# Two attention and MLP layers on one core: the last block of rows for layer 2 is turned by VectorE in 32x32 blocks and through DRAM

## The chip, the cores and the metric

The kernel runs on one core of a Trainium2 chip. The metric is the device time of one execution in microseconds (us), given as the median of several runs. The profile comes from one further execution.

Five engines appear: PE (TensorE: matmuls; PEld is its weight load), DVE (VectorE), ACT (ScalarE), POOL (GpSimd) and SP (SyncE), whose queue issues nearly all DMAs of this kernel. Each engine takes its instructions in the order in which the program lists them, and waits at one whose input is not there.

## What is computed

Two layers are applied twice with the same weights, to x of 2048 rows by 640 columns (S by D), all in float32. There are 32 heads of 20 columns, and the MLP has 1536 hidden columns.

```python
def _A_ref(x, wqkv, wo):                    # attention
    qkv = (x @ wqkv).reshape(B, S, 3, H, Dh).transpose(2, 0, 3, 1, 4)
    q, k, v = qkv[0], qkv[1], qkv[2]
    scores = jnp.einsum("bhqd,bhkd->bhqk", q, k) * (Dh ** -0.5)
    p = _softmax(scores, axis=-1)
    o = jnp.einsum("bhqk,bhkd->bhqd", p, v)
    return o.transpose(0, 2, 1, 3).reshape(B, S, D) @ wo

def _B_ref(x, w1, b1, w2, b2):              # MLP
    r = jnp.maximum(jnp.einsum("bsd,df->bsf", x, w1) + b1, 0)
    return jnp.einsum("bsf,fd->bsd", r * r, w2) + b2

x = x + _A_ref(_layernorm(x), wqkv, wo)
x = x + _B_ref(_layernorm(x), w1, b1, w2, b2)
x = x + _A_ref(_layernorm(x), wqkv, wo)
x = x + _B_ref(_layernorm(x), w1, b1, w2, b2)
```

## The kernel before

**Stages.** `layer` (L1256) is called twice. Each call runs the projections (`qkv`, L674), the attention (L941), the output projection (`add_heads`, L1125) and the MLP (`mlp`, L1195). The 2048 rows are worked on as four blocks (`tb` 0 to 3) of 512 rows, each of them four row tiles of 128 x 640.

**Turned rows.** A projection needs the normalised rows turned, with the 640 columns on partitions: five tiles `xnT` of 128 x 2 x 512, where the middle index is the high and the low part of each number. `xt_[tb]` holds the five tiles of a block. The kernel has two ways to make them:

- `front` (L376): VectorE takes the statistics of four row tiles (`stats`, L239; the last two operations of it, an addition and a power, run on POOL) and normalises them. TensorE then turns them with 20 transposes of 128x128 (L393) into banks of PSUM. Each bank is split into high and low parts, by ACT and VectorE (`split_to`) or by ACT and POOL (`split_on_pool`).
- `turn_out` and `turn_in` (L1146, L1180): VectorE normalises each row tile and turns it in 32x32 blocks (L1172), four DMAs per row tile store the blocks to their turned places in a DRAM tensor `d_t` (`store`, L1156, pieces of 128 bytes), and five DMAs load the turned block back. ACT then copies the high part (L1188) and VectorE subtracts it for the low part (L1189).

For layer 2, the blocks 0, 1 and 2 are turned the second way during the last MLP pieces of layer 1 (L1321 to L1328). Block 3 consists of the rows that this MLP writes last, in four DMAs to `d_x[1]`. Its turning is the generator `second` (L1340), and it is the first way, `front(3, ...)`.

**Projections.** `qkv` works through `UNITS`: first 16 units of queries and keys, four of each block (tb 0, then 1, 2 and 3), then the rest. Unit 0 is the keys of the first heads for block 0, unit 1 their queries, unit 2 keys again. A unit has 30 matmuls (L322) of half the rows of the array each. The halves are issued in pairs, so 15 turns of the inner loop (L890 to L897) issue what one unit needs. The two halves lag each other: unit 0 is complete after turn 30, unit 1 after turn 45, unit 2 after 60, and so on. A complete unit is copied out of PSUM by ACT (L263) and split by POOL (L268, L271) into a tile `ev`. The store of `ev` to `d_qk` (`thrice`, two DMAs of 512 and 256 KB) is put on SP's queue one unit later: that of unit 0 at turn 45, of unit 1 at turn 60, of unit 2 at turn 75. ACT also makes a small mark (L324) after each first half of a unit, for which the second half waits.

**Maxima.** The softmax needs row maxima of the scores. A part of them is put between the projections: `by_queries` (L474) multiplies a tile `q` with a tile `k`, loaded back from `d_qk`, and VectorE reduces the result (L486). The loads of the first `k` and `q` (`tiles`, two DMAs each) go on SP's queue at turn 75, right behind the store of unit 2. The first of these matmuls comes at turn 105, ahead of unit 7's first. The `q` tile holds what unit 1 gave, so its load waits for unit 1's store.

**The order of the steps.** The generator that makes block 3 is asked for its next step (`step_rest`, L826) on every fourth turn of the inner loop. Each step yields a cost in us by which a small model of the engines' times is moved on, and a flag. With the flag set, the next step is made only when two PSUM banks are free. The model decides where the maxima go. `front` has 12 steps, and puts its last transposes on the queues some 50 turns in. If `xt_[3]` is not there when unit 12 is due, all remaining steps are made at once (L887). Unit 12 is the first to use it.

Of the kernel before, what the change touches and what calls it, by code (L numbers as in the profile page):

```python
# [39 lines left out]
def tile_layers(  # L40
# [26 lines left out]
    def slot(shape, dtype, label):  # L67
        return arena.tile(shape, dtype, tag="slot", name=name(label))

    def dma(eng, dst, src):  # L70

        if dst.dtype == F32R:
            dst = dst.bitcast(F32)
        if src.dtype == F32R:
            src = src.bitcast(F32)
        eng.dma_start(dst, src)  # L76

    def xtile(label):
        return xpool.tile([P, D], F32, tag="x", name=name(label))
# [18 lines left out]
    ps_q = Ring(0, 1, 2, 3)  # L98
# [137 lines left out]
    d_t = [dram.tile([D, QB], F32, name=f"d_t{i}") for i in range(5)]  # L236
    d_x = [dram.tile([S, D], F32, name=f"d_x{i}") for i in range(3)]

    def stats(x):  # L239

        st = small.tile([P, 2, 6], F32, tag="bst", bufs=3, name=name("bst"))
        mv = small.tile([P, 2], F32, tag="mv", bufs=6, name=name("mv"))
        for i in range(2):
            nc.vector.bn_stats(st[:, i, :], x[:, i * HALF : (i + 1) * HALF])  # L244
        nc.vector.bn_aggr(mv, st)
        var = mv[:, 1:2]
        nc.gpsimd.tensor_tensor(var, var, eps_t, op=ALU.add)
        nc.gpsimd.tensor_tensor(var, var, half_t, op=ALU.pow)
        return mv

    def normalise(eng, x, mv):
        eng.tensor_scalar(x, x, mv[:, 0:1], mv[:, 1:2], op0=ALU.subtract, op1=ALU.mult)
# [22 lines left out]
    def row_tile(src, r):  # L275
        t = xtile("x")
        dma(nc.sync, t, src[r * P : (r + 1) * P, :])
        return t
# [11 lines left out]
    xt_, keys = {}, {}  # L290
# [85 lines left out]
    def front(tb, x_src, bank, each=1, on_pool=()):  # L376

        rows = [row_tile(x_src, tb * 4 + i) for i in range(4)]
        yield 0, False
        mvs = []  # L380
        for x in rows:
            mvs.append(stats(x))
            yield 1.1, False
        for n, (x, mv) in enumerate(zip(rows, mvs)):
            normalise(nc.vector, x, mv)
            yield 0.65, n == 3
        res = []
        for k0 in range(0, KD, each):
            ks = range(k0, min(k0 + each, KD))
            dsts = [bank("xt") for _ in ks]  # L390
            for k, dst in zip(ks, dsts):
                for i in range(4):
                    nc.tensor.transpose(  # L393
                        dst[:, i * P : (i + 1) * P], rows[i][:, k * P : (k + 1) * P], ident
                    )
            for k, dst in zip(ks, dsts):
                t = slot([P, 2, QB], F32R, "xnT")
                (split_on_pool if k in on_pool else split_to)(t[:, 0, :], t[:, 1, :], dst)
                res.append(t)
            if len(res) == KD:  # L400
                xt_[tb] = res
                rows.clear()
            yield 0, len(res) < KD
# [742 lines left out]
    def turn_out(d, xs):  # L1146

        if callable(xs):
            read, xs = xs, []
            xs.extend(read(i) for i in range(2))  # L1150
        else:
            read = None
        yield
        y = None

        def store(i):  # L1156
            for a in range(4):
                t0 = i * P + 32 * a
                dma(
                    nc.sync,  # L1160
                    d[:, t0 : t0 + 32].rearrange("(b j) t -> j b t", j=32),
                    y[32 * a : 32 * a + 32].rearrange("j (b t) -> j b t", t=32),
                )

        for i in range(4):
            if y is not None:
                store(i - 1)
            mv = stats(xs[i])
            yield
            normalise(nc.vector, xs[i], mv)  # L1170
            y = xtile("y")
            nc.vector.transpose(y, xs[i])  # L1172
            if read and i < 2:
                xs.append(read(i + 2))
            yield
        store(3)
        xs.clear()
        yield

    def turn_in(d, get, sub=nc.vector.tensor_sub):  # L1180

        res = get()
        for k in range(KD):
            dma(nc.sync, res[k][:, 1, :], d[k * P : (k + 1) * P, :])
        yield
        for k in range(KD):
            raw = res[k][:, 1, :].bitcast(F32)
            nc.scalar.copy(res[k][:, 0, :], raw)  # L1188
            sub(res[k][:, 1, :], raw, res[k][:, 0, :].bitcast(F32))  # L1189
            yield  # L1190

    def new_rows():
        return [slot([P, 2, QB], F32R, "xnT") for _ in range(KD)]
# [146 lines left out]
    def second():  # L1340


        yield from front(3, d_x[1], ps_q, 2, (1, 3))

    def constants():

# [57 lines left out]
    opening = begin_first()  # L1404
    next(opening)
    ahead = second()
    layer(True, x_in, d_x[0], d_x[1], opening, ahead)
    layer(False, d_x[1], d_x[2], x_out, ahead, None)
# [28 lines left out]
```

## Time and profile before

| what | us |
|---|---|
| median of three runs | 3612.47 |
| lowest and highest of them | 3610.52, 3614.29 |
| the profiled execution's own time | 3611.78 |
| span of its trace | 3610.0 |
| of it PE busy | 3582.4 |
| of it DVE busy | 2753.2 |
| of it ACT busy | 2640.6 |
| start of layer 2's projections in the trace | 1819.4 |
| first matmul for a maximum in layer 2 (L474) | 1849.6 |

Times in the trace count from the start of the span. The execution's own time stands 1.78 us above its span, and 0.69 us below the median. A row of the timeline gives start, length, engine, line, operation, what is written and read, and the number of instructions merged into it. In brackets stands how long the engine was idle before and what ended that. Lengths of merged rows include short waits between the instructions. "SPq" rows are DMAs being issued; their data moves later.

### The profile page before, as it was taken

How to read it: one execution, taken by the hardware profiler on the slowest of the kernel's cores; microseconds unless marked ns; L12 is line 12 of the kernel's file. 1: busy time of each engine (PE TensorE's matmuls, PEld its weight loads, DVE VectorE, ACT ScalarE, POOL GpSimd, SP SyncE). 2: the span in 40 equal slices, each digit the busy share in tenths (PEclk: the TensorE clock that was granted, in tenths of full speed). 3: DMA queues.
4: the chain of work that ended last, by engine and by line, in shares of the span. 5: the costliest groups of instructions: out<-in, count | busy, mean ns of one | idle time of the engine just before them, and what ended most of it. 6: DMA issues, size and time to landing. Idle time of an engine off the chain costs nothing.

```text
span 3610.0 us, 67661 instructions
## 1 busy us (share of the span) xinstructions
PE 3582.4 (99%) x25550; PEld 2131.8 (59%) x25550; DVE 2753.2 (76%) x5083; ACT 2640.6 (73%) x5131; POOL 820.8 (23%) x904
## 2 busy tenths in 40 slices
PE   8999999999999999999999999999999999999999
PEld 6887334343344335999988964334434343368998
DVE  7877999999999993446567789999999999824443
ACT  2678999999999996122317789999999999942221
POOL 6531334212112111111154201211211211211110
PEclk9999999999999999999999999999999999999999
DMA  8865555322222125834577652222222211367221
GB/s 269 274 228 181 169 146 160 118 69 77 53 53 52 35 91 189 283 88 112 149 253 249 205 151 67 73 73 56 77 72 62 50 39 51 106 212 249 73 79 39
DMA packets 377829, 453.89 MB, mean 126 GB/s; under 512 B 176690, under 2 KB 223538, under 8 KB 377502
## 3 DMA queue, kind: packets, MB, share of 16 engines
q1 hardware_dynamic: 376686, 447.21, 41.2%
q8 instruction: 201, 3.29, 0.4%
q10 hardware_dynamic: 816, 2.36, 0.2%
q14 instruction: 126, 1.03, 0.1%
HBM read 275.14 MB, written 174.30 MB: 125 GB/s over the span
## 4 chain that ended last, share of the span: by engine, by line
PE 95%; DMA 2%; DVE 1%; ACT 1%; issue 1%; SPq 0%; POOL 0%; ACTq 0%; DVEq 0%; POOLq 0%
PE banks L568 28%; PE banks L556 19%; PE banks L474 16%; PE banks L286 12%; PE banks L322 10%; PE banks L1225 9%; PE banks L1066 1%; DMA q<-d_qk 0%; ACT e L563 0%; SPq L76 0%; DMA w<-d_w 0%; PE banks L393 0%; ACT e L1073 0%; DMA d_t<-y 0%; DVE bst L244 0%
## 5 line engine op out<-in xcount | busy, mean ns | idle before, releaser
L563 ACT ACTIVATE e<-banks 128x512 f32<-128x512 f32 x3968 | 2049.1, 603 | 66.0 <-PE banks L474 7.2
L486 DVE TENSOR_REDUCE mx<-banks 128x1 f32<-128x512 f32 x3076 | 1930.9, 684 | 213.4 <-PE banks L474 142.4
L474 PE MATMUL banks<-k,q 60*128 60x512 f32 x3587 | 1244.7, 428 | 2.7 <-DVE mx L486 1.4
L556 PE MATMUL banks<-q,k 62*128 62x512 f32 x3968 | 1117.8, 433 | 1.0 <-DVE mx L503 0.3
L568 PE MATMUL banks<-e,vg 128*32 128x512 f32 x8192 | 1091.8, 605 | 1.5 <-ACT e L1073 1.5
L556 PEld LDWEIGHTS banks<-q,k 62*128 62x128 f32 x3968 | 583.8, 185 | 657.8 <-ACT e L563 625.5
L474 PEld LDWEIGHTS banks<-k,q 60*128 60x128 f32 x3587 | 582.5, 185 | 289.5 <-DVE mx L486 216.1
L503 DVE CUSTOM_DVE_ANT_0 rl<-banks,rl 128x512 f32<-128x512 f32 x511 | 333.6, 689 | 102.1 <-PE banks L474 92.8
L322 PE MATMUL banks<-xnT,wqk 64*128 64x512 f32 x2400 | 383.4, 397 | 4.0 <-DVE xnT L257 1.8
L568 PEld LDWEIGHTS banks<-e,vg 128*32 128x32 f32 x8192 | 161.2, 108 | 357.4 <-issue 330.8
L1210 ACT ACTIVATE r<-banks,b_t 128x512 f32<-128x512 f32 x96 | 66.2, 689 | 398.0 <-PE banks L286 396.6
L495 ACT ACTIVATE rl<-banks 128x512 f32<-128x512 f32 x515 | 273.8, 597 | 102.3 <-PE banks L474 97.4
L1225 PE MATMUL banks<-w,h 128*128 128x320 f32 x2304 | 340.4, 309 | 0.0
L1225 PEld LDWEIGHTS banks<-w,h 128*128 128x128 f32 x2304 | 339.2, 188 | 1.3
L286 PE MATMUL banks<-xnT,w 128*128 128x512 f32 x1440 | 329.4, 389 | 0.0
L322 PEld LDWEIGHTS banks<-xnT,wqk 64*128 64x128 f32 x2400 | 289.7, 187 | 39.4 <-issue 2.2
L286 PEld LDWEIGHTS banks<-xnT,w 128*128 128x128 f32 x1440 | 269.6, 188 | 55.3
L268 POOL CAST mr<-nt 128x32 fp32r<-128x32 f32 x64 | 13.5, 211 | 1125.8 <-DVE nt L529 1125.7
L612 POOL TENSOR_TENSOR few<-few,minus_t 128x16 f32<-128x16 f32 x62 | 179.9, 2902 | 234.4 <-DMA few<-d_s 232.7
L322 PE MATMUL banks<-wv,xnT 64*128 64x320 f32 x1920 | 199.7, 307 | 0.9 <-ACT mark_t L324 0.9
L322 PEld LDWEIGHTS banks<-wv,xnT 64*128 64x128 f32 x1920 | 187.9, 185 | 2.7 <-ACT mark_t L324 1.6
L1211 DVE TENSOR_TENSOR r<-r 128x512 f32<-128x512 f32 x96 | 77.7, 809 | 124.7 <-ACT r L1210 124.6
(82 smaller groups left out, 2010.6 us busy)
## 6 DMA issues: line engine op xcount, KB each, us to landing
q<-d_qk SPq DMA_DIRECT2D x242, 240.0 KB
d_qk<-ev SPq DMA_DIRECT2D x80, 512.0 KB
k<-d_qk SPq DMA_DIRECT2D x152, 240.0 KB
x<-d_x SPq DMA_DIRECT2D x88, 320.0 KB
d_qk<-ev SPq DMA_DIRECT2D x80, 256.0 KB
d_o<-ot SPq DMA_DIRECT2D x248, 80.0 KB
ot<-d_o SPq DMA_DIRECT2D x38, 512.0 KB
d_v<-v SPq DMA_DIRECT2D x32, 512.0 KB
```

The source lines that it names most:

```text
L286: nc.tensor.matmul(dst, a, b, start=(n == 0), stop=(n == last))
L322: m = nc.tensor.matmul(ch["dst"][:, :width], *pair, start=first, stop=last)
L474: nc.tensor.matmul(dst, q_t[t][b : b + 60, p, sub * P : (sub + 1) * P], k_t[t // NQB, c][b : b + 60, p, :], start=True, stop=True,)
L486: nc.vector.tensor_reduce(maxima(t)[:, 2 * par + p, sub, c : c + 1], dst, axis=AX.X, op=ALU.max)
L495: nc.scalar.activation(res, dst, AF.Relu)
L503: nc.vector.tensor_tensor_reduce(out=r, in0=dst, in1=r, scale=1.0, scalar=LEAST, op0=ALU.add, op1=ALU.max, accum_out=maxima(t)[:, 2 * par ...
L556: nc.tensor.matmul(dst, k_t[t // NQB, kt // 4][b : b + 62, p, (kt % 4) * P : (kt % 4 + 1) * P], q_t[t][b : b + 62, p, :], start=True, stop ...
L563: nc.scalar.activation(es[p][:, par, :], dst, AF.Exp, scale=SCALE)
L568: nc.tensor.matmul(acc[32 * h : 32 * h + 32, :], v_t[t // NQB, kt // 8][:, kt % 8, 32 * h : 32 * h + 32], es[p][:, par, :], start=(kt == 0 ...
L612: nc.gpsimd.tensor_tensor(few, few, minus_t, op=ALU.pow)
L1211: nc.vector.tensor_mul(r, r, r)
L1225: nc.tensor.matmul(dst[:, :HALF], hs[f][:, hx, i * P : (i + 1) * P], w_2.piece(at_2(f0 + f, hw, hf)), start=(f == 0 and (hx, hw) == THREE[0]),
```

## The change

`second` no longer calls `front`. Block 3 is turned in the way of the other three blocks. The steps are spread over the same turns of the inner loop, one on every fourth turn.

```diff
     def second():
-        yield from front(3, d_x[1], ps_q, 2, (1, 3))
+        rows_out = turn_out(d_t[0], lambda i: row_tile(d_x[1], 12 + i))
+        for n, _ in enumerate(rows_out):
+            yield (0 if n in (0, 9) else 1.1 if n % 2 else 1.5), False
+        for _ in range(3):
+            yield 0, False
+        res = []
+
+        def get():
+            res.extend(new_rows())
+            return res
+
+        rows_in = turn_in(d_t[0], get)
+        next(rows_in)
+        for _ in range(6):
+            yield 0, False
+        for _ in rows_in:
+            yield 0.7, False
+        xt_[3] = res
+        yield 0, False
```

The new `second` has 25 steps, all with the flag off. With one step on every fourth turn, they fall as follows:

| turn | step |
|---|---|
| 4 | two row loads |
| 8, 16, 24, 32 | statistics of row tiles 0 to 3; those at 16, 24 and 32 are preceded by the four stores of the tile before |
| 12, 20, 28, 36 | normalise and turn row tiles 0 to 3; row loads 2 and 3 at turns 12 and 20 |
| 40 | the four stores of row tile 3 |
| 44, 48, 52 | nothing |
| 56 | the five loads of the turned block |
| 60 to 76 | nothing |
| 80, 84, 88, 92, 96 | one ACT copy and one VectorE subtraction each |
| 100 | `xt_[3]` is set |

## The prediction

> **What bounds the kernel now.** I read the page first.
>
> ```profile
> PE 3582.4 (99%) x25550; PEld 2131.8 (59%) x25550; DVE 2753.2 (76%) x5083; ACT 2640.6 (73%) x5131; POOL 820.8 (23%) x904
> PE 95%; DMA 2%; DVE 1%; ACT 1%; issue 1%; SPq 0%; POOL 0%; ACTq 0%; DVEq 0%; POOLq 0%
> ```
>
> PE is busy nearly always and holds 95% of the chain that ended last. So a stretch that PE loses or gains ends up in the total, unless something else then holds PE up. The change touches the first units of layer 2's projections. The table by windows, for the projection matmuls alone, shows PE's time there.
>
> ```profile
> 1819.30:1829.07 9.77, 9.20 (x72) 6.78 (x72) 1.00 0.47 168
> 1829.07:1836.07 7.00, 3.20 (x22) 1.72 (x20) 1.00 0.30 115
> 1836.07:1849.36 13.29, 13.29 (x118) 10.98 (x119) 1.00 0.63 204
> ```
>
> The columns are the window, its length, busy time of PE and PEld with counts, granted clock, DMA share and GB/s. The timeline of PE fills in the middle window.
>
> ```profile
> 1829.08 0.64 PE L393 MATMUL banks<-ident,x 128*128 128x128 f32 x3
> 1830.21 0.77 PE L393 MATMUL banks<-ident,x 128*128 128x128 f32 x5 [0.49 <-DVE x L252]
> 1830.90 0.50 PE L322 MATMUL banks<-xnT,wqk 64*128 64x512 f32 x2
> 1831.33 1.09 PE L393 MATMUL banks<-ident,x 128*128 128x128 f32 x8
> 1832.36 0.73 PE L322 MATMUL banks<-xnT,wqk 64*128 64x512 f32 x4
> 1833.02 0.66 PE L393 MATMUL banks<-ident,x 128*128 128x128 f32 x4
> 1833.60 1.89 PE L322 MATMUL banks<-xnT,wqk 64*128 64x512 f32 x13
> 1836.07 1.20 PE L322 MATMUL banks<-xnT,wqk 64*128 64x512 f32 x8 [0.58 <-ACT r L263]
> ```
>
> The 20 transposes, the waits between them and the late copy of a unit (0.58 us, ACT was busy with the turned banks) fill the window beside 19 projection matmuls (2+4+13).
>
> **What it removes.** A projection matmul takes 13.29/118 = 0.113 us, so 19 take 2.1 us of the 7.0. The rest, **4.9 us**, is PE time that goes with the transposes. PE would then come to the first matmul for a maximum (turn 105) at 1849.4 - 4.9 = 1844.5. This is worth something only if that matmul's data is there. In the kernel before it is just there:
>
> ```profile
> 1838.09 0.88 SPq L76 DMA_DIRECT2D d_qk<-ev  x2
> 1842.25 0.80 SPq L76 DMA_DIRECT2D d_qk<-ev  x2
> 1843.21 1.38 SPq L76 DMA_DIRECT2D k<-d_qk  x2
> 1844.71 0.85 SPq L76 DMA_DIRECT2D q<-d_qk  x2
> 1849.58 0.39 PE L474 MATMUL banks<-k,q 60*128 60x512 f32 x1
> 1850.21 0.69 PE L474 MATMUL banks<-k,q 60*128 60x512 f32 x3 [0.24 <-DMA q<-d_qk]
> ```
>
> The stores are those of units 1 and 2. The query tile's two halves are issued from 1844.71 to 1845.56, and the second ends a wait of PE at 1850.2. So **the query load is already next in line** behind PE, and the question is what the change does to it.
>
> **What it adds: the row chain.** One row tile's period on VectorE is seen where the second way runs with little else between:
>
> ```profile
> 1451.58 0.87 DVE L244 BATCH_NORM_STATS2 bst<-x 128x6 f32<-128x320 f32 x2
> 1455.42 0.86 DVE L244 BATCH_NORM_STATS2 bst<-x 128x6 f32<-128x320 f32 x2
> 1456.32 0.21 DVE L245 BATCH_NORM_AGGREGATE mv<-bst 128x2 f32<-128x12 f32 x1
> 1456.45 0.44 DVE L1140 TENSOR_TENSOR x<-banks,x 128x320 f32<-128x320 f32 x1
> 1457.46 0.61 DVE L252 TENSOR_SCALAR x<-x,mv 128x640 f32<-128x640 f32 x1 [0.57 <-POOL mv L248]
> 1458.11 0.85 DVE L1172 STREAM_TRANSPOSE y<-x 128x640 f32<-128x640 f32 x1
> 1823.55 0.89 DVE L244 BATCH_NORM_STATS2 bst<-x 128x6 f32<-128x320 f32 x2 [3.57 <-DMA x<-d_x]
> ```
>
> The period is 3.84 us. Of the two additions of L1140 in it, the one after a transpose costs 0.38 and the one after the aggregate lies under the wait for POOL, so here it is 3.46 us, and 3.54 us from statistics to the end of the transpose. The rows come as before, the first at 1823.55, because the row loads keep their place on SP. The last transpose ends at 1823.55 + 3 x 3.46 + 3.54 = 1837.5. All this lies under PE, and VectorE has no maxima yet, so it costs nothing by itself.
>
> **The stores and loads on SP.** Rows from the MLP of layer 1:
>
> ```profile
> 1773.20 1.98 SPq L76 DMA_DIRECT2D d_t<-y  x4
> 1775.29 4.76 SPq L76 DMA_DIRECT2D xnT<-d_t  x10
> 1774.00:1776.45 2.45, 2.45 (x19) 2.45 (x18) 1.24 (x3) 0.00 (x0) 0.00 (x0) 1.00 0.93 136
> 1776.45:1785.40 8.95, 8.95 (x44) 7.64 (x44) 1.88 (x3) 1.87 (x3) 0.00 (x0) 1.00 1.01 359
> ```
>
> The four stores of a row tile take 2.0 us to issue, and their data has moved 3.25 us after the first issue (1773.20 to 1776.45), 80 KB each at a mere 136 GB/s.
>
> Here the last four are issued 1837.5 to 1839.5 and have landed by about 1841.0 (3.25 and some 0.2 for the signal). Unit 0's store (turn 45) goes out between. Then come the five loads (turn 56), which need all sixteen stores. **SP waits at the first of them until 1841.0**, and issues the five by 1843.4 (4.76/10 each). Queued behind them on SP are, in this order: unit 1's store, unit 2's store, the first k and q. Before, unit 1's store went out at 1838.09. Now it goes out at 1843.4, though its tile is ready at about 1838 (POOL works on unit 0 only after the third tile's power, but that ends at 1832.5, and the units follow at 2 us each).
>
> **The query load.** It needs unit 1's store landed, and the data of all these DMAs shares the same 16 engines in order. The rate is seen where they queue:
>
> ```profile
> 1843.00:1850.10 7.10, 6.97 (x62) 5.43 (x58) 0.06 (x1) 1.69 (x6) 4.85 (x5) 1.00 0.98 309
> 1850.10:1862.00 11.90, 10.76 (x87) 9.89 (x89) 10.97 (x19) 1.98 (x5) 10.02 (x12) 1.00 0.98 334
> ```
>
> So 309 to 359 GB/s; I take 335. From 1840.75: unit 0's store (786 KB, 2.35 us), five loads (1311 KB, 3.9), unit 1's store (2.35) to 1849.3, unit 2's (2.35), k (492 KB, 1.45) to 1853.1, the first half of q (246 KB, 0.75) to 1853.9. At 359 and 309 GB/s it is 1853.0 and 1855.0. Against 1849.4 the first maximum's matmul is **3.6 to 5.6 us late; I take 4.4**, near the middle, as both rates occur within one stretch. The gain of 4.9 is eaten, since PE waits from 1844.5 to about 1853.8. ACT's five copies (turns 80 to 96) wait for the loads and hold the marks and copies of units 4 to 6 behind them, which would stop PE for some 2 us. That lies under the longer wait.
>
> **The clock.** Nine idle microseconds of PE have one more price. The table by windows shows a shorter one in layer 1:
>
> ```profile
> 83.95:87.36 3.41, 1.40 (x12) 1.36 (x14) 1.06 (x2) 1.43 (x4) 2.02 (x3) 1.00 1.04 344
> 87.36:90.77 3.41, 3.41 (x19) 3.19 (x18) 2.24 (x6) 0.44 (x1) 0.00 (x0) 0.50 1.00 381
> 90.77:94.19 3.42, 3.42 (x30) 3.24 (x30) 2.79 (x6) 1.78 (x4) 1.03 (x2) 1.00 1.06 266
> ```
>
> After a stretch of 3.41 us with PE busy for 1.40, the granted clock is 0.50 for the next one, and back at 1.00 after it; 19 matmuls ran instead of 30. The Trainium skill, "TensorE: Matmul & The Clock Gate", Part 1, halves the clock after at least one idle window of about 3.4 us; here 2.0 idle of 3.41 did it. By that page's 3.4 us to full clock, the loss would be an estimated 1.7 us.
>
> PE restarts inside a stretch at half speed, and that one or the next as well is slow: 0 to 5.4 us at half, a loss of 0 to 2.7. Behind it stands a DMA queue that is full (0.98 at 334 GB/s above) and holds PE up anyway at one place:
>
> ```profile
> 1860.16 0.47 PE L474 MATMUL banks<-k,q 60*128 60x512 f32 x1 [0.92 <-DMA q<-d_qk]
> ```
>
> That wait shrinks when PE is slow. I take 1.2 us net.
>
> **What changes nothing.** The steps after turn 105 are the same, since both generators have ended by then and the model's engines are idle again. The tb 3 tiles are ready near 1848.5 and first used by unit 12, which started at about 1874: no stall. Four transposes and three more subtractions on VectorE lie in a stretch where it is mostly idle; if maxima were there, they would cost up to 4 x 0.85 + 2 x 0.7 us.
>
> **Sum.** 3611.78 + 4.4 + 1.2 = 3617.4 for an execution like the profiled one. That one is 0.7 us under the median, so for the median I say **3618.0**. The bounds are +3.6 to +5.6, and 0 to +2.7, so 3616 to 3621.
>
> **Rivals.**
>
> 1. *The cover holds.* If the loads do not hold up the queue so, because SP gets past them early or their data moves beside unit 1's store, the query comes when unit 2's store lets it. That could be 2.2 us earlier than before (POOL done at 1840 and not 1842.2), or as early as PE wants it, 4.9. Time 3607.6 to 3610.3. For it: the DMA engines were empty for much of 1826 to 1843. The Trainium skill, "DMA: Bandwidth & Descriptors", Rules for kernel authors, says to issue a DMA early, compute, and wait late, as the fixed cost overlaps; by that rule this rival wins. Against it: the loads wait on SP, and issue is not early for what stands behind them. 15%.
> 2. *No difference.* The delay just equals what PE had lost: the query comes at 1849 to 1851, with a short cold stretch. Time 3611 to 3614. It needs the row chain to end 3 us sooner than I have it; VectorE's rows above speak against that. 12%.
> 3. *Slower still.* After the wait, the full DMA queue never makes up, and PE at half speed for two stretches loses 2.7 with no wait to absorb it. The next query tile is late too, by 1 to 3 us. Time 3611.8 + 5.6 + 2.7 + 1 to 3 + 0.7 = 3622 to 3624. It decides when the restart falls late in a stretch and the queue stays at 0.98 up to 1890. 20%.
> 4. *It does not do what it says*: block 3 is needed before it is there, and all steps are forced together ahead of unit 12. Unit 12 is due 25 us after the tiles, so under 1%.
>
> **Chances.** My forecast, 3614 to 3622 with its own slack, has 53%. From 3610 to 3623 leaves out most of the first rival and half of the third, about 2 in 10. The bound of 0.2% (7.2 us, about what a measurement of this kernel can tell from no change) lies at 3605.3 and 3619.7. Faster than that needs more than all of PE's gain: 0.04. Slower: the third rival and the upper quarter of the forecast, 0.33. The rest, 0.63, is within.
>
> **What would show it.** In the changed kernel, right would be: no L393 in layer 2; the last transpose near 1837.5; SP's loads `xnT<-d_t` near 1841, unit 1's store after them; PE idle of 8 to 10 us ahead of the first L474, ended by DMA q; a granted clock of 0.50 in the windows right after. It would be wrong if unit 1's store went out near 1838, if L474 came by 1846, or if ACT's copies, and not the query, ended PE's wait.

## The result, and the profile after

| | kernel before | changed kernel |
|---|---|---|
| median of 15 runs each, us | 3612.36 | 3619.1 |
| lowest and highest | 3607.55, 3618.24 | 3615.76, 3622.17 |
| span of the profiled execution | 3610.0 | 3617.3 |

The ratio is 1.002, with a 95% interval of 1.0012 to 1.0027: the change costs 6.7 us, between 4.3 and 9.8. The range of 3610 to 3623 holds it, and 3618.0 was forecast. A second series of the changed kernel, later and beside other kernels, gave 3619.41 against 3613.5, ratio 1.0018 (1.0009 to 1.0027).

The page of the changed kernel shows what was traded. PE lost 2.9 us of busy time, and the packets under 512 bytes grew from 176690 to 187266:

```profile
PE 3579.5 (99%) x25530; PEld 2127.8 (59%) x25530; DVE 2758.3 (76%) x5089; ACT 2639.6 (73%) x5131; POOL 815.3 (23%) x900
DMA packets 389045, 456.51 MB, mean 126 GB/s; under 512 B 187266, under 2 KB 234114, under 8 KB 388718
```

In this execution layer 2's projections start at 1816.2, against 1819.4 in the trace of before. The programs are the same up to there; the trace of before has two short stretches at half clock in layer 1 that this one lacks. So times are compared from each trace's own first projection matmul of layer 2. SP's rows in the changed kernel:

```profile
1834.86 2.14 SPq L76 DMA_DIRECT2D d_t<-y  x4
1837.11 0.95 SPq L76 DMA_DIRECT2D d_qk<-ev  x2
1839.01 2.27 SPq L76 DMA_DIRECT2D xnT<-d_t  x5
1841.33 0.94 SPq L76 DMA_DIRECT2D d_qk<-ev  x2
1842.37 2.49 SPq L76 DMA_DIRECT2D d_qk<-ev  x2
1844.95 2.21 SPq L76 DMA_DIRECT2D k<-d_qk  x2
1848.59 0.78 SPq L76 DMA_DIRECT2D q<-d_qk  x2
```

These are the last row tile's stores, unit 0's store, the five loads, the stores of units 1 and 2, the first k and the first q, in the order that the program gives. The query load goes out 32.4 us after the start (1848.59 - 1816.2); before it was 25.3 (1844.71 - 1819.4). What SP waited for between 1815 and 1849, with the total in us, the number of waits and the longest:

```profile
SPq L76 <- DVE y L1172: 8.9, 4, 5.4
SPq L76 <- DMA d_qk<-ev: 1.3, 1, 1.3
SPq L76 <- DMA d_t<-y: 0.8, 1, 0.8
```

The stores wait for VectorE's turned tiles, the loads for the stores, and the query load for unit 1's store to land. SP's queue is taken in order, so each of these waits also holds what stands behind it. PE's timeline around it, and the one further wait of note:

```profile
1828.81 13.89 PE L322 MATMUL banks<-xnT,wqk 64*128 64x512 f32 x119 [0.61 <-ACT r L263]
1853.38 1.77 PE L474 MATMUL banks<-k,q 60*128 60x512 f32 x4 [10.68 <-DMA q<-d_qk]
1885.76 0.54 PE L474 MATMUL banks<-kd,q 60*128 60x512 f32 x1 [1.88 <-DMA q<-d_qk]
```

PE is done with its seven units at about 1842.7 and waits 10.7 us for the query. The first maximum's matmul comes at 37.2 us after the start, against 30.2 before. The table by windows shows the stretch, with the granted clock before the last two columns:

```profile
1842.60:1845.06 2.46, 0.10 (x1) 0.00 (x0) 1.29 (x2) 0.62 (x1) 0.00 (x0) 1.00 0.98 287
1845.06:1853.35 8.29, 0.00 (x0) 0.00 (x0) 3.13 (x4) 2.79 (x7) 6.68 (x7) 0.50 1.03 348
1853.35:1858.71 5.36, 5.33 (x23) 4.11 (x25) 3.85 (x7) 0.00 (x0) 0.99 (x1) 0.50 1.02 402
1858.71:1883.90 25.19, 24.94 (x211) 21.27 (x207) 24.29 (x41) 4.09 (x12) 12.87 (x14) 1.00 0.94 294
1883.90:1886.00 2.10, 0.24 (x2) 0.27 (x4) 0.28 (x1) 0.00 (x0) 1.61 (x2) 1.00 1.01 380
1886.00:1889.40 3.40, 3.40 (x18) 3.08 (x18) 0.70 (x2) 1.19 (x2) 0.00 (x0) 0.50 1.02 402
```

The DMA engines are full (0.94 to 1.03) the whole time, also while PE stands still. The clock is halved from 1845.06 to 1858.71, 5.4 us of it after PE's restart, and once more after the short wait.

### The profile page after: what moved, and what is told of

It is laid out like the page before. It is cut to its first block, busy times and chain, and to the rows that moved or that the text cites. A ratio compares the mean times of both kernels' runs of the same rounds, so it can differ in the third digit from the quotient of the medians.

```text
span 3617.3 us, 67664 instructions
## 1 busy us (share of the span) xinstructions
PE 3579.5 (99%) x25530; PEld 2127.8 (59%) x25530; DVE 2758.3 (76%) x5089; ACT 2639.6 (73%) x5131; POOL 815.3 (23%) x900
## 2 busy tenths in 40 slices
DMA packets 389045, 456.51 MB, mean 126 GB/s; under 512 B 187266, under 2 KB 234114, under 8 KB 388718
## 3 DMA queue, kind: packets, MB, share of 16 engines
q14 instruction: 126, 1.03, 0.1%
## 4 chain that ended last, share of the span: by engine, by line
PE 55%; DMA 2%; issue 1%; SPq 1%; POOL 0%; DVE 0%; ACT 0%; POOLq 0%; DVEq 0%; ACTq 0%
PE banks L568 14%; PE banks L286 10%; PE banks L556 10%; PE banks L1225 9%; PE banks L474 8%; PE banks L322 5%; SPq L76 1%; DMA w<-d_w 1%; DMA d_t<-y 0%; DMA q<-d_qk 0%; DMA d_qk<-ev 0%; DMA d_x<-x 0%; DMA xnT<-d_t 0%; DMA o<-d_r 0%; DVE x L1140 0%
## 5 line engine op out<-in xcount | busy, mean ns | idle before, releaser
L474 PE MATMUL banks<-k,q 60*128 60x512 f32 x3587 | 1245.4, 429 | 12.3 <-DMA q<-d_qk 10.9
L568 PE MATMUL banks<-e,vg 128*32 128x512 f32 x8192 | 1091.0, 605 | 1.5 <-ACT e L1073 1.5
L474 PEld LDWEIGHTS banks<-k,q 60*128 60x128 f32 x3587 | 582.9, 185 | 299.9 <-DVE mx L486 217.1
L568 PEld LDWEIGHTS banks<-e,vg 128*32 128x32 f32 x8192 | 161.1, 108 | 357.5 <-issue 331.0
```

The lines of the kernel that those rows point to most:

```text
L474: nc.tensor.matmul(dst, q_t[t][b : b + 60, p, sub * P : (sub + 1) * P], k_t[t // NQB, c][b : b + 60, p, :], start=True, stop=True,)
L568: nc.tensor.matmul(acc[32 * h : 32 * h + 32, :], v_t[t // NQB, kt // 8][:, kt % 8, 32 * h : 32 * h + 32], es[p][:, par, :], start=(kt == 0 ...
```

## The experiments

The theory at this point: the stores and loads of the turned block stand in the DMA queue ahead of the first query tile, so PE waits for the query, and the transposes that it saved are worth nothing. Rivals: SP's order and not the bytes; ACT held at the copies; the halved clock.

All results in one table. "First maximum" and "attention" are the first L474 and the first L568 of layer 2, in us after its first projection matmul (from the source views of each trace, good to 0.1 us). Medians and ratios are against the kernel before in the same series.

| kernel | first maximum | attention | median, us | before, us | ratio, 95% interval |
|---|---|---|---|---|---|
| before | 30.2 | 296.9 | | | |
| changed | 37.2 | 307.8 | 3619.1 | 3612.36 | 1.002, 1.0012 to 1.0027 |
| changed, again | 37.3 | 306.0 | 3619.41 | 3613.5 | 1.0018, 1.0009 to 1.0027 |
| loads behind q | 33.2 | 305.3 | 3616.49 | 3611.56 | 1.0013, 1.0004 to 1.0021 |
| loads between | 37.2 | 306.0 | 3620.81 | 3611.56 | 1.0025, 1.0015 to 1.0036 |
| copies late | 36.7 | 307.3 | 3620.86 | 3611.56 | 1.0025, 1.0016 to 1.0034 |
| PE kept busy | 37.4 | 305.6 | 3620.14 | 3611.56 | 1.002, 1.001 to 1.003 |
| no turning | 26.2 | 294.5 | 3606.77 | 3612.52 | 0.9982, 0.9973 to 0.9991 |
| no stores | 31.0 | 299.6 | 3612.28 | 3612.52 | 1.0004, 0.9996 to 1.0013 |
| no loads | 32.5 | 301.3 | 3614.49 | 3612.52 | 1.001, 1.0001 to 1.0019 |
| PE work added | 34.5 | 300.8 | 3612.85 | 3612.52 | 1.0003, 0.9994 to 1.0012 |
| front spaced | 30.4 | 298.1 | 3612.45 | 3613.5 | 0.9995, 0.9987 to 1.0004 |
| last stores behind q | 29.5 | 303.7 | 3620.28 | 3613.5 | 1.0018, 1.0009 to 1.0027 |
| subtractions on POOL | 29.2 | 303.5 | 3614.83 | 3611.65 | 1.0012, 1.0003 to 1.0021 |

An interval is some 6 us wide, and each trace is one execution. So the places of the loss are read from the traces, and totals are compared only where intervals part.

**Loads behind the query.**

```diff
-        for _ in range(3):
+        for _ in range(8):
...
-        for _ in range(6):
+        for _ in range(10):
...
-            yield 0.7, False
+            yield 0, False
```

> The five loads of the turned block go on SP's queue at turn 76, behind the first k and q, and the copies at turns 120 to 136; the copies' cost in the model is 0, so that PE's order stays as it was. Theory (the loads stand ahead of unit 1's store and the first query load): the first maximum's matmul comes 27 to 29.5 us after layer 2's first projection matmul (30.2 before the change, 37.2 after it), no half clock; the time is 3 us under to 3 us over the kernel before, so 4 to 10 under the changed one. Rival (the loads' bytes have to pass the full DMA queue somewhere, whatever their place): the first matmul is early too, but later query loads are late by 4 us, and the time is 5 to 7 us over the kernel before.

The first maximum came at 33.2, about half way back and 3.7 us later than the latest expected. (With ten steps between, the copies fall on turns 116 to 132.) The time was 4.9 us over the kernel before, close to the rival. SP's rows and PE's waits in that kernel:

```profile
1836.12 2.14 SPq L76 DMA_DIRECT2D d_t<-y  x4
1838.36 4.66 SPq L76 DMA_DIRECT2D d_qk<-ev  x6
1843.19 1.85 SPq L76 DMA_DIRECT2D k<-d_qk  x2
1845.15 0.89 SPq L76 DMA_DIRECT2D q<-d_qk  x2
1846.08 2.37 SPq L76 DMA_DIRECT2D xnT<-d_t  x5
...
1850.53 0.76 PE L474 MATMUL banks<-k,q 60*128 60x512 f32 x1 [6.73 <-DMA q<-d_qk]
...
1884.96 0.47 PE L474 MATMUL banks<-kd,q 60*128 60x512 f32 x1 [1.33 <-DMA q<-d_qk]
```

Even with the loads out of the way, the query goes out at 27.9 (1845.15 - 1817.3) and not at 25.3. The stores, which were still ahead, keep it back, by their bytes or by SP's waits for them.

**Loads between the stores of units 1 and 2.** As above, with `range(5)` for the first number, and the second left at 6.

> The loads go on SP's queue at turn 64, behind unit 1's store but ahead of unit 2's store, k and q; the copies' cost in the model is 0. If the bytes ahead of the query in the DMA queue set its landing: q lands at most 1.5 us earlier than in the changed kernel, first maximum's matmul 35.5 to 37.5 us after the first projection matmul, time within 2 us of the changed kernel. If it is the late store of unit 1, for which the query load waits on SP: 32.5 to 35 us, and 3 to 5 us under the changed kernel.

The store of unit 1 and the query both went out earlier, and the first maximum came at 37.2 as in the changed kernel. The wait of PE and the DMA engines' load over it, with the same window of the changed kernel below:

```profile
1855.56 0.76 PE L474 MATMUL banks<-k,q 60*128 60x512 f32 x1 [10.64 <-DMA q<-d_qk]
1842.00:1855.50 13.50, 2.92 (x25) 2.06 (x22) 5.59 (x6) 4.10 (x9) 7.83 (x7) 0.71 1.02 327
```

```profile
1839.90:1853.30 13.40, 2.80 (x25) 1.99 (x21) 4.51 (x6) 4.03 (x9) 6.63 (x7) 0.69 1.01 322
```

So whether unit 1's store stands ahead of the loads or behind them on SP is not what counts. The bytes ahead of the query are the same, and they move at 322 to 327 GB/s. The stores stand in the same place in both kernels, so nothing is shown here of their order.

**Copies late.** The loads stay at turn 56; the wait of six steps becomes `range(15)`, and the copies' cost 0.

> The loads stay at turn 56, the ACT copies and VectorE subtractions go from turns 80 to 96 to turns 116 to 132, behind the first maximum; their cost in the model is 0. Theory: PE's wait is for the query load, so it stays at 10 to 11 us, and the time within 1.5 us of the changed kernel. Rival (ACT, held at the copies, holds the marks and the bank copies for which PE waits): PE's wait shrinks by 2 us or more, and so does the time.

```profile
1856.34 2.09 PE L474 MATMUL banks<-k,q 60*128 60x512 f32 x4 [10.25 <-DMA q<-d_qk]
```

The wait stays, 0.4 us shorter. In the changed kernel ACT was held for 5.28 us at the first copy, but nothing of PE's waited for it in the end. This rival falls.

**PE kept busy.**

```diff
         xt_[3] = res
+        for _ in range(72):
+            nc.tensor.transpose(banks[:, 2, :P], ident, ident)
         yield 0, False
```

> The changed kernel with 72 transposes of the identity into an unused bank at turn 100, some 9.8 us of PE work with no use, so that PE is not idle in its wait. Theory: the halved clock behind the wait costs time of its own; the granted clock stays 1.00, and the time is 2 to 3.5 us under the changed kernel. Rival (PE has nothing to do at that point but wait for the full DMA queue, so its clock costs nothing): within 1 us of the changed kernel.

The first half of the expectation missed: PE still stood idle for 2.7 us, and one stretch at half speed followed. The windows of this kernel:

```profile
1844.80:1853.40 8.60, 8.60 (x77) 7.90 (x75) 5.51 (x6) 3.67 (x7) 5.21 (x5) 1.00 0.98 340
1853.40:1856.00 2.60, 0.03 (x2) 0.00 (x0) 0.00 (x0) 0.67 (x2) 2.30 (x3) 1.00 1.03 306
1856.00:1857.60 1.60, 1.34 (x9) 0.93 (x11) 1.00 (x2) 0.00 (x0) 0.20 (x1) 1.00 1.08 425
1857.60:1861.10 3.50, 3.50 (x20) 2.87 (x18) 3.31 (x6) 0.00 (x0) 0.00 (x0) 0.52 1.01 400
```

From the first maximum to the attention it took 268.2 us, against 268.7 and 270.6 in the two traces of the changed kernel, so 0.5 to 2.4 us less. The median is no better than the changed kernel's. A price of the clock between nothing and some 2 us stays open.

**No turning.** The kernel before, with `xt_[3] = list(xt_[2])` in place of `front`.

> The kernel before, with block 3 of layer 2 not turned at all: its projections use block 2's tiles, and the row loads, statistics, transposes and splits of block 3 are left out. It bounds what any cheaper turning can give. If PE's time sets the end of this stretch: about 4.9 us under the kernel before. Theory, sharpened by the first runs (the full DMA queue sets the pace of the first 90 us, so PE's time there is worth little): first maximum's matmul 28 to 30 us after the first projection matmul, and the time 0 to 3 us under the kernel before.

PE arrives at 26.2, before the 28 to 30 that was expected, and hardly waits. The time falls by 5.8 us (3.3 to 9.8), more than the theory gave and close to the 4.9 of the rival. So PE's time there is worth something when nothing is put into the DMA queue for it. This kernel also does without the row loads and the work of VectorE and POOL, so not all of the 5.8 need be PE's.

**Stores or loads alone.** The changed kernel without the sixteen stores, and without the five loads with their copies and subtractions.

> The changed kernel without the sixteen stores of the turned blocks; the loads stay and bring what an earlier block left in the DRAM tensor. It takes 1.3 MB in pieces of 128 bytes, some 10 us of the DMA engines, out of the stretch ahead of the query load. Theory of the DMA queue: first maximum's matmul at 31 to 34 us after the first projection matmul (37.2 with the stores), time 1 to 4 us over the kernel before. If the loads alone are the cost: 36 to 37 us, and 5 to 8 us over the kernel before.

> The changed kernel without the five loads, five copies and five subtractions of the turned block; the stores stay, and block 3's projections use block 2's tiles. Theory of the DMA queue: first maximum's matmul near 33 us, as with the loads behind the query (33.2), but no later query load is held up by them, so 1 to 4 us over the kernel before. If the stores cost nothing: first maximum's matmul 28 to 30 us, and the time not over that of the kernel before.

PE's first wait for the query in either, stores left out first:

```profile
1848.62 0.76 PE L474 MATMUL banks<-k,q 60*128 60x512 f32 x1 [4.54 <-DMA q<-d_qk]
```

```profile
1848.78 2.05 PE L474 MATMUL banks<-k,q 60*128 60x512 f32 x4 [5.92 <-DMA q<-d_qk]
```

Against the changed kernel (37.2), **leaving out the stores brings the first maximum 6.2 us forward, and leaving out the loads 4.7**. With either alone it still comes later than in the kernel before (31.0 and 32.5 against 30.2). So either uses up the 4.0 us that PE gains, and neither total parts from the kernel before to the faster side.

Counted from the kernel without turning (26.2), the delays are 4.8 for the loads, 6.3 for the stores and 11.0 for both. That the first two add up to the third does not show that each is time of bytes in one queue, for two reasons. First, POOL finishes unit 1's tile at different times. Its rows for units 0 and 1 in the changed kernel, and below them for unit 1 without turning:

```profile
1829.99 1.41 POOL L271 TENSOR_TENSOR ev<-kf,ev 128x512 fp32r<-128x512 f32 x1
1833.69 1.42 POOL L271 TENSOR_TENSOR ev<-r,ev 128x512 fp32r<-128x512 f32 x1
```

```profile
1830.58 1.29 POOL L271 TENSOR_TENSOR ev<-r,ev 128x512 fp32r<-128x512 f32 x1
```

Unit 1's tile, for whose store the query waits, is ready 18.9 us after the start in the changed kernel (1835.11 - 1816.2), as it is with either part left out, but 14.6 us without turning (1831.87 - 1817.3), where POOL has no statistics to wait for. A kernel with the work on rows, but neither stores nor loads, was not run.

Second, the stores act through SP's order too. In the changed kernel unit 0's tile is ready at 1831.40, but its store goes out at 1837.11, behind the stores that SP holds for VectorE. The DMA engines are not full up to there:

```profile
1826.00:1837.10 11.10, 10.49 (x91) 8.35 (x89) 6.80 (x12) 2.13 (x6) 7.35 (x11) 1.00 0.73 123
```

So how much of the stores' 6.2 us is their bytes, and how much the pile-up behind SP's waits, these runs do not show.

**PE work added.** The kernel before, with sixteen empty steps after `front` and then 36 transposes of the identity.

> The kernel before with 36 transposes of the identity into an unused bank at turn 104, right ahead of the first maximum: 4.9 us of PE work with no use, about what the change takes away. If PE sets the pace of the stretch: 4 to 5 us over the kernel before. Theory of the DMA queue: first maximum's matmul 34 to 35.5 us after the first projection matmul, but PE then waits less for the later query loads, and the time is 0 to 2.5 us over the kernel before.

The first maximum came 4.3 us later, the time by 0.3 us (from 2.2 less to 4.3 more). The trace has the attention 3.9 us later. Together with the kernel without turning, this does not settle how much a microsecond of PE is worth here; it lies between none and all.

**Front spaced.**

```diff
-        yield from front(3, d_x[1], ps_q, 2, (1, 3))
+        for n, (cost, _) in enumerate(front(3, d_x[1], ps_q, 1)):
+            yield cost, False
+            if n == 8:
+                for _ in range(3):
+                    yield 0, False
```

> The kernel before, still with TensorE's transposes, but three empty steps ahead of them, one bank on every fourth turn, flags off, and all low parts by VectorE instead of two by POOL. PE no longer waits for VectorE's normalising nor for the late bank copy, some 1.7 of the 4.9 us; the rest is the 20 transposes and stays. Theory (each saved microsecond ahead of turn 105 counts only as far as the query load comes earlier as well, and POOL now is freer for units 0 to 2): first maximum's matmul 27.5 to 29.5 us after the first projection matmul (30.2 before), time 0.5 to 3 us under the kernel before. Rival (the query load stays where it was): 30 us, and no difference.

No difference, in place or in time (ratio 0.9995, 0.9987 to 1.0004). PE's timeline shows why:

```profile
1833.76 0.65 PE L393 MATMUL banks<-ident,x 128*128 128x128 f32 x4
1834.35 1.19 PE L322 MATMUL banks<-xnT,wqk 64*128 64x512 f32 x8
1835.47 0.66 PE L393 MATMUL banks<-ident,x 128*128 128x128 f32 x4
1836.06 1.19 PE L322 MATMUL banks<-xnT,wqk 64*128 64x512 f32 x8
1837.18 0.66 PE L393 MATMUL banks<-ident,x 128*128 128x128 f32 x4
```

There are no waits, yet the period of four transposes and eight projection matmuls is 1.71 us. Eight matmuls are 0.9 of it (8 x 0.113), so four transposes cost 0.8 us and twenty cost 4.0. The waits that I counted in the kernel before were not on top of that.

**Last stores behind the query.**

```diff
             yield (0 if n in (0, 9) else 1.1 if n % 2 else 1.5), False
-        for _ in range(3):
+            if n == 8:
+                for _ in range(9):
+                    yield 0, False
+        for _ in range(5):
...
-            yield 0.7, False
+            yield 0, False
```

> The changed kernel with the last row tile's four stores at turn 76, behind unit 2's store, k and q on SP's queue, the five loads at turn 100 and the copies from turn 124; their cost in the model is 0. The first three row tiles' stores stay ahead. If the stores cost through SP's order (the last ones wait there for VectorE's transpose, ahead of unit 0's store): first maximum's matmul 26.5 to 28.5 us after the first projection matmul. If through their bytes, some 7 of 10 us of DMA time still ahead: 30 to 32 us. In both cases the loads come later into the full queue, and the time ends 0 to 5 us over the kernel before.

The first maximum came at 29.5, a little before that of the kernel before. This is between the two cases. Against the kernel with stores and no loads (32.5), the last tile's four stores cost 3.0 us by standing ahead of the query. That does not part the two: their bytes are out of the way, but SP also has one transpose less to wait for, and unit 0's store goes out 17.2 us after the start and not 20.8. The time was 6.8 us over the kernel before. A new wait stood 12 us on, put down to VectorE, whose subtractions now stood among the maxima:

```profile
1846.89 1.89 PE L474 MATMUL banks<-k,q 60*128 60x512 f32 x4 [2.99 <-DMA q<-d_qk]
...
1863.42 0.50 PE L474 MATMUL banks<-k,q 60*128 60x512 f32 x1 [4.10 <-DVE mx L468]
```

**The same, with the subtractions on POOL.** The call becomes `turn_in(d_t[0], get, nc.gpsimd.tensor_sub)`.

> The kernel with the last stores and the loads behind the query, and the five subtractions of the turned block by POOL instead of VectorE. There, PE's second wait (4.1 us) ended with VectorE, whose subtractions stood among the maxima. If VectorE was the cost: the second wait falls under 1.5 us and the time to 1 to 4 us over the kernel before. If the loads in the full DMA queue were: a wait of 3 us or more stays, now ended by the DMA of a query or key tile, and the time stays 5 to 8 us over the kernel before.

```profile
1843.48 2.03 PE L474 MATMUL banks<-k,q 60*128 60x512 f32 x4 [2.69 <-DMA q<-d_qk]
...
1860.17 0.47 PE L474 MATMUL banks<-k,q 60*128 60x512 f32 x1 [4.04 <-DMA q<-d_qk]
```

With VectorE out of it, the second wait is as long and ends with the next query tile. So **the transfers put behind the first query are waited for at the second**: 2.7 and 4.0 us, where the changed kernel waits 10.7 us at once. The time, 3.2 us over the kernel before, lies in the range that was expected if VectorE was the cost, but its interval does not part it from the kernel ahead of it. So the wait speaks for the queue, and the total does not decide. No version that was run beats the kernel before, save the one that leaves the turning out.

## Why the prediction was right, and where it was not

- *The gain of 4.9 us on PE* was about 4.0: the kernel without turning reaches its first maximum 26.2 us after the start, not 30.2. The 4.9 counted waits that the spaced kernel shows to be no extra, and one wait for a bank copy (0.61 us) stayed.
- *The row chain* held. From the first projection matmul, the last transpose was due at 18.1 and ended at 18.7; two of the four normalisings took 0.88 us and not 0.61.
- *SP waits at the loads* held as an event (the loads went out at 22.8, due at 21.6, and unit 1's store at 25.1, due at 24.0). The loads went out 4.15 us after the first of the last four stores (1839.01 - 1834.86), where the prediction had 3.25 and some 0.2 for the signal; no run shows that 0.2 by itself. As a cause unit 1's place behind the loads counted for nothing: with its store moved ahead of them, the first maximum came no sooner. That SP waits at the stores, and unit 0's store behind them, has a share that is not measured.
- *"3.6 to 5.6 us late; I take 4.4"* is the step that failed in size. It was 7.0 us (37.2 against 30.2), beyond its own upper end. The query load itself went out at 32.4 and not at 29.9, where the prediction has unit 1's store landed (1849.3 - 1819.4), and these 2.5 us are nearly all of the difference. Parts of it are the loads' start, 1.2 us after its due time, and the lower rate: 322 GB/s and not 335 makes 0.5 us on the 4.4 MB that the prediction counted. The rest is not broken up.
- *The clock, 1.2 us net*: it was halved as foreseen, for 5.4 us after the restart, the upper end. What that cost is not settled: the DMA engines were full at 1.02 in that time, and keeping PE busy for most of the wait took 0.5 to 2.4 us off the stretch up to the attention and nothing off the median. The Trainium skill, "TensorE: Matmul & The Clock Gate", Part 1, asks for an idle window of about 3.4 us. The clock fell after 2.4 us of idleness here (1842.7 to 1845.06), so the measurement differs from the page.
- *What changes nothing* held: the order of PE's matmuls is the same in both programs but for the transposes, and unit 12 did not wait for its tiles.
- *Sum*: +5.5 forecast, +6.7 measured (4.3 to 9.8). The traces put the stretch up to the attention 9 to 11 us longer (306.0 and 307.8 against 296.9). The later query wait of the third rival is part of it: 1.88 us in the first of the two traces. Why that is more than the medians show stays open; the trace of before is one execution out of a spread of 10 us. So the total came out well, in part by luck: the query's delay was 2.6 us too small, the clock's term is not measured, and a wait that the forecast had left to a rival came on top.
- *The first rival*, a hidden transfer, fell. The Trainium skill, "DMA: Bandwidth & Descriptors", Rules for kernel authors, advises issuing early and waiting late, as the fixed setup cost overlaps. No run here shows that cost by itself. The traces show that issuing early does not hide time in a queue that others wait in: the loads stand 24 turns ahead of the first copy, and with them left out the query's matmul comes 4.7 us sooner.

## What to carry to other kernels

Work moved from PE to the DMA engines is free only if the queue has room where its bytes pass. Look up the next load that a busy engine waits for, and add up the bytes ahead of it at the rate that the windows show. Look also at what the issuing queue itself waits for, as a store that waits for its tile holds all that is listed behind it. Here, moving the transfers to another place in a full queue changed which load was late, and no such kernel ended sooner than the kernel before.

## What the runs showed of the hardware that was not expected

- The query's matmul came 4.7 us sooner without 1.3 MB of loads ahead of it, and 6.2 us sooner without 1.3 MB of stores in pieces of 128 bytes (and SP's waits for them). Putting one store ahead of those loads or behind them made no difference (37.2 us in both).
- Twenty 128x128 transposes in float32, set between projection matmuls without any wait, cost PE 0.2 us each, more than the 0.136 us at which eight of them followed each other (1.09 us in the trace of before).
- PE's clock was halved for four stretches of 3.41 us on end (13.65 us) after one wait. In the kernel that kept PE busy, 2.6 idle microseconds were enough for one such stretch.
